# Joining the two output visits of a block on TensorE: chunked scan and gated MLP on one core

## The chip, the core and the metric

One core of a Trainium2 chip runs the whole program. The metric is device time in microseconds (us) for one execution; lower is better. Three runs of the kernel before took 336.29, 338.03 and 337.85 us, median 337.85.

## What is computed

A decayed linear-attention scan over 4 batches, 8 heads, 768 positions, head size 32 and state size 16 is followed by a gated MLP over the 3072 tokens (256 wide, 1536 hidden), all in float32. Cut to what matters:

```python
for c in range(nc):                      # chunks of 32 in the reference, pieces of 64 in the kernel
    cum = np.cumsum(la, axis=-1)
    L = np.exp(cum[:, :, :, None] - cum[:, :, None, :]) * causal
    M = np.einsum('bhin,bhjn->bhij', Cc, Bc) * L
    y_intra = np.einsum('bhij,bhjd->bhid', M, xc)
    y_inter = np.einsum('bhin,bhnd->bhid', Cc, state) * np.exp(cum)[:, :, :, None]
    y[:, :, sl] = y_intra + y_inter
    state = decay_full[:, :, None, None] * state + np.sum(Bx, axis=2)
...
g = x @ w_gate
return (g * sigmoid(g) * (x @ w_val)) @ w_out
```

## The kernel before, in words

The 768 positions are six blocks of 128 (numbered `k` from 0 in the code, so block two is `k == 1`), each of two pieces of 64. For a block, decays, B, C and x are loaded; VectorE scans the decays into `L` and `E`; TensorE computes state sums (`sums`) and scores (`scores`), in one visit for blocks two to five; VectorE multiplies scores by decays (`mix`) and carries the state on (`step`); then TensorE computes the block's outputs (`outputs`, which is `values`, decayed values from `L` and `x`, and then `carried`, the carried state against C). The result goes into four PSUM banks `y` and is copied out as the MLP's input, split into a high and a low part because the wide matmuls run in a reduced float32 form with two parts for each operand.

The outputs of a batch are 32 passes of values (64 rows by 32 columns of the array, 64 columns moved) and 16 passes of carried state (32 by 64, 64 moved); a float32 matmul is two passes, each with a weight load of its own. A block has four batches: 128 and 64 passes, 192 in all. Before, `outputs` runs twice for a block, for batches 0 and 1 and for batches 2 and 3, with a pause of 2.6 us of planner time between, in which TensorE takes other work.

That other work is the MLP: for a block 12 groups of gate and value matmuls (`gv`, 512 columns) and 12 of output matmuls (`po`). Block four's groups 4 to 11 are `halved` and blocks five and six together form a `PAIR`, both with fewer multiplications by means of mixed weights (`ws`, `wos`), which the kernel makes on the chip (`mix_weights`, `mix_out`), writes to DRAM (`keep`) and fetches again (`fetch_mixed`, `fetch_out`).

The order of the work on every engine comes out of a list scheduler, `Plan`, that runs on the host: each operation has a cost, a rank (about its due time, smaller goes first), what it needs and which buffers it takes. The order of each engine, and of the SP queue that issues the DMAs, is then fixed. The settings that the change touches stand near the end of the file: `LEAD[k]` is how far ahead of its MLP work a block's scan is ranked (`z` in the code), `LATER` how late the first nine weights are cast, `MAKE` and `MAKE_STEP` when the mixed gate weights are made, `OUT_MAKE` and `OUT_STEP` the same for the output weights, `AHEAD` how far ahead of use mixed weights are fetched, and `URGENT` the rank of the copies and sums between the halved block's terms. `IDLE` gives dummy passes (`idle`) that write a bank nobody reads: 22 of 128 columns at the very start, and a few of 512 columns in block one.

All engine calls are recorded at one line (L202, a helper), so rows are told apart by their tiles: `y<-L,xb` is `values`, `y<-bc,T` is `carried`, `st` and `S` are state sums and scores, `rest` is a dummy.

Of the kernel before, what the change touches and what calls it, by code (L numbers as in the profile page):

```python
# [17 lines left out]
BATCH, H, S, D, N = 4, 8, 768, 32, 16  # L18
DM, DFF = 256, 1536
P = 128  # L20
# [4 lines left out]
T = BATCH * P  # L25
# [18 lines left out]
class Plan:  # L44
# [26 lines left out]
    def add(self, engine, cost, run, rank, needs=(), takes=(), uses=(), gives=None, kind=None, lag=0.0, rows=1.0, slack=0.0):  # L71
        engines = [(engine, cost)] if cost is not None else engine
        self.ops.append(Op(engines, run, rank, needs, takes, uses, gives, kind, lag, rows, slack))
# [139 lines left out]
def scan_moe_kernel(ctx: ExitStack, tc, rows, decays, bc, xb, wgv, wo, cst, out):  # L213
# [763 lines left out]
    def gate_val(k, f, m):  # L977
        t = hid.setdefault((k, f), {})["gv"[m]] = ps_mm.tile([P, T], F32, tag="mm", name=f"gv{k}_{f}_{m}")
        if not k and f < WHOLE:
            w = part[f]["w"].bitcast(F32).rearrange("p (a b c) -> p a b c", b=2, c=P)  # L980
# [59 lines left out]
    def idle(n, i):  # L1040

        if not n and not i:
            rest[0] = ps_at.tile([P, T], F32, tag="at", name="rest")
        c = T if n else P
        wide = dn.rearrange("p g t -> p (g t)").bitcast(BF16)[:, :c] if n else one[:, :c]
        te.matmul(rest[0][:, :c], one[:, :P], wide, start=True, stop=True)

# [11 lines left out]
    def do(f, *a):  # L1059
        return lambda *e: f(*a, *e)  # L1060
# [6 lines left out]
    add = plan.add  # L1067
# [4 lines left out]
    def units(k, n):  # L1072
        return GV * n - (GV - GVH) * max(n - HALVED.get(k, NF), 0)

    for k in range(NB):
        begin[k] = t
        if k == PAIR:
            begin[k + 1], begin_sum[k], begin_sum[k + 1] = t, t + PAIR_LAG, t + NF * (GVP + PO)
            break
        t += (units(k, NF) if k else WHOLE * PACE0 + (NF - WHOLE) * GV) + ATT  # L1080
        for i in (() if not k else (0, 1) if k == 1 else (k,)):
# [3 lines left out]
    def due(k, f=0):  # L1085

        if k in HALVED:
            return begin[k] + units(k, f)
        return begin[k] + f * (GV if k else PACE0) - (0 if k else max(f - WHOLE, 0) * (PACE0 - GV))

# [6 lines left out]

    for n, ranks in enumerate(IDLE):
        for i, r in enumerate(ranks):
            need = [("idle", n, i - 1)] if i else [("idle", n - 1, len(IDLE[n - 1]) - 1)] if n else []  # L1100
            if n:
                need = need + [(("S", 0, BATCH - 1), ("vals", 0), ("y", 0))[n - 1]]
            takes = [] if i or n else [("at", "rest")]
            c = T if n else P
            add("PE", 0.2133 * c / T, do(idle, n, i), r, need, takes=takes, uses=["rest"], gives=("idle", n, i), kind="r")


    for i in range(NW):
# [8 lines left out]
        add("DVE", 0.6, do(w_round, i), r - 3.3 if i else -0.94, [("shift", i), ("rest", i), *([] if i else [("ce", 0)])], uses=[("raw", i)], gives=("round", i))  # L1117
        early = WHOLE <= i < NF
        if i < NF and not early:
            r = due(1, i) - LATER  # L1120
        later = [("M", 1, NP - 1)] if i < WHOLE else []
        add([("Act", 0.525), ("DVE", 0.34)], None, do(w_high, i), r - 2.7, [("round", i), *later], gives=("wh", i))
        whole_done = [("gv", 0, i, m) for m in range(2)] if i < WHOLE else []
        add("DVE", 0.6, do(w_low, i), r - 1.5, [("wh", i), *whole_done], uses=[("w", i)], gives=("wl", i))
# [9 lines left out]
    for k in range(NB):  # L1134
        r = due(k)
        SLACK = min(k / 2, 1.0)
        z = -5 if not k else r + LEAD[k]
        L, E, BC, XB, CZ, TT = ("L", k), ("E", k), ("bc", k), ("xb", k), ("Cz", k), ("T", k)
# [16 lines left out]
        if not k:  # L1155
# [3 lines left out]
            for b in range(BATCH + 1):  # L1159
                for i in range(2 if b < BATCH else 1):  # L1160
# [7 lines left out]
                    need = [t, ("decays", 0), "dj"] + ([("scan0", b - last_one)] if i else []) + ([("M", 0, NP - 2)] if b == BATCH else [])  # L1168
# [15 lines left out]
        y = [("y", k, i) for i in range(2 * K)]  # L1184
        for bs in [(b,) for b in range(BATCH)] if not k else [range(BATCH)]:
            b, more = bs[-1], bs[0]
            n = len(bs)
            stb = st[:1] if k in ST_ONE else st
            bank = "mm" if k in ST_MM else "at"
            if k in JOINED:  # L1190
# [3 lines left out]
                need = [*(("bt", k, i) for i in bs), ("Cz", k)]  # L1194
# [11 lines left out]
        for q in range(0 if k else 1, len(st)):  # L1206
            need = [*before, ("E", k), ("ap", k, q)] + ([] if k or q > 1 else [("ap", k, 0), ("round", 2)])
            add("DVE", 0.785, do(step, k, q), z + (8 if k else 25) + q, need, uses=[] + ([("T", k - 1)] if k and not q else []), gives=("step", k, q))
            before = [("step", k, q)]
        uses = [L, E, XB, BC, *y, TT]  # L1210
# [3 lines left out]
        for g in range(0 if k else 2):  # L1214
            need = [("M", 0, p) for p in (2 * g, 2 * g + 1)]
            add("PE", 0.45, do(values, 0, range(BATCH), (g,)), -1.4 + 0.1 * g, need, takes=[("mm", y[2 * q + g]) for q in range(K)], uses=[L, XB, *y], gives=("vals", g), kind="f")
        if k:
            need = [*(("M", k, p) for p in range(NP)), ("ce", k), *steps]
            add("PE", 1.52, do(outputs, k, (0, 1)), z + 11, need, takes=[("at", i) for i in y], uses=y, gives=("y", k, 0), kind="f", slack=min(k - 0.5, 2.5))
            add("~", 2.6, lambda: None, z, [("y", k, 0)], gives=("pause", k))  # L1220
            add("PE", 1.52, do(outputs, k, (2, 3)), z + 11, [("pause", k)], uses=[L, *uses], gives=("y", k), kind="f")
        for b in range(0 if k else BATCH):
            add("PE", 0.135, do(carried, 0, b), -1, [("vals", 0), ("vals", 1), ("ce", 0), *steps], uses=uses, gives=("y", 0) if b == BATCH - 1 else ("y", 0, b), kind="f")
        done = [("y", k)]
# [71 lines left out]
    for r in range(NF // 2):  # L1296
        at = OUT_MAKE + OUT_STEP * r
        i = NF + r
        u = [("sg", ("out", r, n)) for n in range(2)]
        add("DVE", 0.6, do(whole_again, r), at, [("wl", i), ("wh", i), ("round", NW - 1), MIXED_AFTER, *prior], takes=u, gives=("ws", i, -1))  # L1300
        uses = [key for _, key in u]
# [6 lines left out]
    for k in (*HALVED, PAIR):  # L1308
        for f in user(k):
            other = in_raw(f) if k == PAIR else f in LOOSE.get(k, ())  # L1310
            need = [("spared", f), *behind, *(["new_t1", "new_t2"] if other and k == PAIR else [("xtl", k, 1)] if other else [])]
# [9 lines left out]
    def stay_home(r, n):  # L1321
        home = HOMES[r][STAYS.index(n)]
        if home == "sg":
            return [("sg", ("stay", r, n))], []
        if home[0] == "wg":
            return [], [("term", home[1], i) for i in (1, 2, 4)]
        return [], [("spare", *home[:2])]
# [4 lines left out]
    for f in range(NF):  # L1332
        r = due(PAIR, f)
        c = 0.681
# [25 lines left out]
        for b in range(2):  # L1360
            home, need = stay_home(f // 2, f"{f % 2 + 1}{b + 1}")
# [3 lines left out]
    for r in range(R):  # L1365
        at = due(PAIR, 2 * r + 1) + SUM_LAG
        pr = [("pr", PAIR + b, 2 * r + o) for b in range(2) for o in range(2)]
        for n, (t, *_) in enumerate((("t1",), ("t3",), ("t2",), ("t4",))):
            home, need = stay_home(r, t) if t != "t3" else ([], [])
            add("DVE", 0.6, do(stay_sum, r, n), at + n * 0.1, [*(pr if not n else [("ksum", r, n - 1)]), *need], takes=home, gives=("ksum", r, n))  # L1370

    at = due(PAIR) + 60.0
# [6 lines left out]
    for j, (n, r) in enumerate(first):  # L1379
        x = TERMS[n][0]  # L1380
        need = [("ksum", r, {"11": 0, "t3": 1, "t1": 2, "22": 2}.get(x, 3)), *([("split", j - 1)] if j else [])]
        tag = "sg" if j % (HB + MORE) >= HB else None
        lh = ("lh", r, x)
        takes = [("sg", lh), ("sg", (lh, 2))] if tag else [("hh", lh)]
# [11 lines left out]
    for j, (n, r, h) in enumerate(steps):  # L1396
# [3 lines left out]
        need = [("lh", r, x), ("ll", r, x), *gate[n], *([prev] if prev else []), *([("osum", r)] if n not in (1, 2, 4) else [])]  # L1400
        takes = [("at", tile_of[b])] if n in (1, 5) and not r or b == "q" and r == R - 2 else []
        uses = [tile_of[b]]
# [10 lines left out]
    for n, k, m, c0, c1, need in (("x", PAIR, 0, 0, T, (2, end, None)), ("z", PAIR + 1, 0, 0, T, (3, end, None)), ("y0", PAIR, 1, 0, T // 2, (4, end, 0))):  # L1413
        c = 0.6 * (c1 - c0) / T
# [47 lines left out]
    for k in range(NB):  # L1462
# [3 lines left out]
        for f in range(NF):  # L1466
            r = due(k, f)
            need = [*xs, ("wh", f), ("wl", f)]
            c = 1.362
            if not k:  # L1470
                need = [("round", f), *(("xf", i) for i in range(2 * K)), ("idle", len(IDLE) - 1, len(IDLE[-1]) - 1)]
                c = 1.717
                if f >= WHOLE:
                    need = [("wh", f), ("wl", f), *(("xh", 0, g) for g in range(2)), *(("xl", 0, g) for g in range(2))]
                    c = 1.362
# [20 lines left out]
        for n, (m, t, fs) in enumerate(sums_of(k) if k < PAIR else []):  # L1496
            b = ("po", k, m, t)
            need = [x for f in fs for x in (("hl", k, f), *([("hl", k, f, 0)] if in_halves(k, f) else []), ("wh", NF + f // 2), ("wl", NF + f // 2))]
# [3 lines left out]
            c = (0.681 if t[1] - t[0] == T else 0.71) * len(fs) * (t[1] - t[0]) / T  # L1502
            add("PE", c, do(project, k, m, t, fs), r, need, takes=[] if fs[0] else [("mm" if k < PAIR else "at", b)], uses=[b, *(("h", k, f) for f in fs)], gives=prev, kind="r")
            if fs[-1] == NF - 1:
                o = ("ob", k, m, t)
                c = 0.6 * (t[1] - t[0]) / T
# [5 lines left out]

CST = W + 2 + 2 * D + 2 * P
NA = NB * K * BATCH * H // P
IDLE = [-9.0] * 22, [-1.45] * 4, [-1.35] * 2, [1000.0] * 3
LATER = 2.4
ST_ONE, ST_MM, JOINED = (), (1, 2, 3, 4), (1, 2, 3, 4)
LEAD = {1: -26.4, 2: -36, 3: -65.3, 4: -66.7, 5: -56.2}
PAIR_LAG, MIXED, RAW = 5.0, 4, 4
MIXED_AFTER = ("y", 1)  # L1520
HALVED = {3: 4}
HALF_AT = "z"
MAKE, MAKE_STEP = 116.9, 3.3
LOOSE = {3: (3, 5, 7)}
AHEAD, URGENT = 14.6, 60


def in_raw(f):
    return f >= MIXED and f % 2 == 0


OUT_MAKE, OUT_STEP = 198.7, 3.7
OUT_RAW = 1, 3, 5
BEHIND, AFTER = 0.9, 0
MORE = 3
# [18 lines left out]
def in_halves(k, f):  # L1554
    return f >= HALVED.get(k, NF)


WHOLE = 9
LATE = {2: NF + 2}
GATE, HASTE = dict(bc=0, aj=0, xb=0, an=1), 7  # L1560
# [53 lines left out]
```

## Time and profile before

| what | us |
|---|---|
| profiled execution, its own time | 335.66 |
| its span, first to last instruction | 333.9 |
| TensorE matmul busy | 328.6 |
| VectorE busy | 295.4 |
| ScalarE busy | 193.4 |
| three runs | 336.29, 337.85, 338.03 |

The profile is of one execution. Busy times of engines lie beside each other; TensorE's weight loads are counted apart and overlap its matmuls. A matmul's duration runs from its start to its modelled end, and many small ones are under way at once, so the distance between starts says more than a duration.

### The profile page before, as it was taken

How to read it: one execution, taken by the hardware profiler on the slowest of the kernel's cores; microseconds unless marked ns; L12 is line 12 of the kernel's file. 1: busy time of each engine (PE TensorE's matmuls, PEld its weight loads, DVE VectorE, ACT ScalarE, POOL GpSimd, SP SyncE). 2: the span in 40 equal slices, each digit the busy share in tenths (PEclk: the TensorE clock that was granted, in tenths of full speed). 3: DMA queues.
4: the chain of work that ended last, by engine and by line, in shares of the span. 5: the costliest groups of instructions: out<-in, count | busy, mean ns of one | idle time of the engine just before them, and what ended most of it. 6: DMA issues, size and time to landing. Idle time of an engine off the chain costs nothing.

```text
span 333.9 us, 7899 instructions
## 1 busy us (share of the span) xinstructions
PE 328.6 (98%) x3186; PEld 258.4 (77%) x3189; DVE 295.4 (88%) x576; ACT 193.4 (58%) x359; POOL 4.1 (1%) x11
## 2 busy tenths in 40 slices
PE   8999999999999999999999999999999999999996
PEld 7644548888888888878888889998888888888785
DVE  6999999987997999888999975998578999989994
ACT  3696898275554653454454445543565556554982
POOL 1300000000000000000000000000000000000000
PEclk9999999999999999999999999999999999999999
DMA  7789659992001598378977489443046511330011
GB/s 249 269 266 340 196 158 381 296 240 52 14 33 34 166 281 345 102 279 234 293 228 291 168 275 222 160 132 125 2 127 251 191 57 71 125 126 0 1 66 63
DMA packets 21261, 57.68 MB, mean 173 GB/s; under 512 B 2280, under 2 KB 3304, under 8 KB 21224
## 3 DMA queue, kind: packets, MB, share of 16 engines
q1 hardware_dynamic: 20808, 56.94, 52.6%
q8 instruction: 25, 0.41, 0.5%
q10 hardware_dynamic: 416, 0.23, 0.2%
q14 instruction: 12, 0.10, 0.1%
HBM read 41.23 MB, written 15.93 MB: 171 GB/s over the span
## 4 chain that ended last, share of the span: by engine, by line
PE 96%; DMA 1%; ACT 1%; issue 0%; DVE 0%; SPq 0%; DVEq 0%; ACTq 0%
PE gv L202 35%; PE po L202 20%; PE py L202 7%; PE y L202 5%; PE px L202 5%; PE oy L202 4%; PE hy L202 3%; PE pz L202 2%; PE pr L202 2%; PE ox L202 2%; PE S L202 2%; PE hz L202 2%; PE hx L202 2%; DMA bc<-in_bc 1%; PE st L202 1%; PE oz L202 1%
## 5 line engine op out<-in xcount | busy, mean ns | idle before, releaser
L202 ACT CAST hh<-sg 128x512 fp32r<-128x512 f32 (+1 forms) x54 | 29.3, 558 | 33.2 <-PE po L202 24.2
L202 DVE TENSOR_TENSOR hl<-sg,hh 128x512 fp32r<-128x512 f32 (+1 forms) x56 | 33.7, 616 | 7.8 <-ACT hh L202 7.3
L202 ACT ACTIVATE sg<-gv 128x512 f32<-128x512 f32 x40 | 23.7, 593 | 24.6 <-PE gv L202 21.3
L202 DVE TENSOR_TENSOR sg<-gv,sg 128x512 f32<-128x512 f32 x40 | 27.5, 687 | 3.2 <-PE gv L202 3.2
L202 DVE TENSOR_TENSOR_SCAN L<-L,dj 128x520 f32<-128x520 f32 x20 | 24.2, 1232 | 0.0
L202 DVE TENSOR_TENSOR ws<-ws 128x128 f32<-128x128 f32 (+1 forms) x60 | 20.2, 369 | 0.1
L202 DVE TENSOR_TENSOR L<-S,L 128x512 f32<-128x512 f32 x24 | 15.8, 689 | 1.1 <-PE S L202 1.1
L202 ACT ACTIVATE sg<-px 128x512 f32<-128x512 f32 x12 | 7.2, 599 | 15.7 <-PE px L202 15.7
L202 PE MATMUL py<-xht,ws 128*128 128x512 f32 x48 | 15.3, 400 | 0.0
L202 DVE TENSOR_TENSOR hlt<-stt,hht 128x512 fp32r<-128x512 f32 x18 | 11.7, 690 | 0.9 <-ACT hht L202 0.7
L202 PEld LDWEIGHTS y<-L,xb 64*32 64x32 f32 x768 | 8.7, 105 | 4.6 <-issue 3.4
L202 ACT ACTIVATE sg<-pz 128x512 f32<-128x512 f32 x12 | 7.2, 599 | 7.2 <-PE pz L202 7.2
L202 ACT ACTIVATE Cz<-bc,cs 128x512 f32<-128x512 f32 x12 | 8.0, 717 | 5.2 <-DMA bc<-in_bc 5.2
L202 ACT CAST ws<-ws 128x512 fp32r<-128x512 f32 x11 | 6.9, 623 | 7.1 <-DVE ws L202 7.0
L202 PE MATMUL y<-L,xb 64*32 64x64 f32 x768 | 10.8, 224 | 0.1
L202 PEld LDWEIGHTS py<-xht,ws 128*128 128x128 f32 x48 | 8.6, 188 | 2.7 <-DVE pz L202 1.2
L202 DVE TENSOR_TENSOR ps<-py,ps 128x512 f32<-128x512 f32 x12 | 8.3, 690 | 2.6 <-PE py L202 2.6
L202 ACT CAST hht<-stt 128x512 fp32r<-128x512 f32 x17 | 9.8, 621 | 0.7 <-DVE stt L202 0.6
L202 PE MATMUL py<-xlt,ws 128*128 128x512 f32 x24 | 9.3, 389 | 0.0
L202 DVE TENSOR_TENSOR pz<-py,ps 128x512 f32<-128x512 f32 x12 | 8.3, 696 | 0.6 <-PE py L202 0.3
L202 ACT COPY py<-px 128x512 f32<-128x512 f32 x12 | 6.9, 574 | 1.3
L202 PE MATMUL y<-bc,T 32*64 32x64 f32 x352 | 7.6, 223 | 0.0
(788 smaller groups left out, 978.8 us busy)
## 6 DMA issues: line engine op xcount, KB each, us to landing
ws<-keep SPq DMA_DIRECT2D x20, 512.0 KB, 4.2
keep<-ws SPq DMA_DIRECT2D x12, 512.0 KB, 6.3
L<-clipped SPq DMA_DIRECT2D x10, 520.0 KB, 9.5
xb<-in_xb SPq DMA_DIRECT2D x6, 768.0 KB, 7.7
bc<-in_bc SPq DMA_DIRECT2D x6, 512.0 KB, 9.7
ws<-uncut SPq DMA_DIRECT2D x12, 256.0 KB, 3.9
wos_k<-keep SPq DMA_DIRECT2D x6, 512.0 KB, 4.3
out<-ob SPq DMA_DIRECT2D x8, 256.0 KB, 2.9
```

The source lines that it names most:

```text
L202: ins = getattr(self.engine, name)(*a, **k)
```

## The change

Blocks two, four, five and six (`MERGED = 1, 3, 4, 5`) compute their outputs of all four batches in one planned operation of 192 passes: 128 of values, then 64 of carried state. Block three keeps two visits with the pause. The dummies at the start are 17 of 164 columns. Eight settings have new values.

```diff
-        c = T if n else P
+        c = T if n else WARM[1]
...
-            add("PE", 1.52, do(outputs, k, (0, 1)), z + 11, need, takes=[("at", i) for i in y], uses=y, gives=("y", k, 0), kind="f", slack=min(k - 0.5, 2.5))
-            add("~", 2.6, lambda: None, z, [("y", k, 0)], gives=("pause", k))
-            add("PE", 1.52, do(outputs, k, (2, 3)), z + 11, [("pause", k)], uses=[L, *uses], gives=("y", k), kind="f")
+            takes = [("at", i) for i in y]
+            if k in MERGED:
+                add("PE", 2.64, do(outputs, k, range(BATCH)), z + 11, need, takes=takes, uses=[L, *uses], gives=("y", k), kind="f", slack=min(k - 0.5, 2.5))
+            else:
+                add("PE", 1.52, do(outputs, k, (0, 1)), z + 11, need, takes=takes, uses=y, gives=("y", k, 0), kind="f", slack=min(k - 0.5, 2.5))
+                add("~", 2.6, lambda: None, z, [("y", k, 0)], gives=("pause", k))
+                add("PE", 1.52, do(outputs, k, (2, 3)), z + 11, [("pause", k)], uses=[L, *uses], gives=("y", k), kind="f")
...
-IDLE = [-9.0] * 22, [-1.45] * 4, [-1.35] * 2, [1000.0] * 3
-LATER = 2.4
+WARM = 17, 164
+IDLE = [-9.0] * WARM[0], [-1.45] * 4, [-1.35] * 2, [1000.0] * 3
+LATER = 3.7
-LEAD = {1: -26.4, 2: -36, 3: -65.3, 4: -66.7, 5: -56.2}
+LEAD = {1: -26.4, 2: -36.0, 3: -72.0, 4: -78.0, 5: -56.2}
-MAKE, MAKE_STEP = 116.9, 3.3
+MAKE, MAKE_STEP = 114.2, 3.3
-AHEAD, URGENT = 14.6, 60
+AHEAD, URGENT = 12.5, 50.5
-OUT_MAKE, OUT_STEP = 198.7, 3.7
+OUT_MAKE, OUT_STEP = 208.5, 5.4
+MERGED = 1, 3, 4, 5
```

## Rows read from the trace of the kernel before

**Rows 1.** The page, parts 1 and 2: busy times, and granted clock in 40 slices.

```profile
PE 328.6 (98%) x3186; PEld 258.4 (77%) x3189; DVE 295.4 (88%) x576; ACT 193.4 (58%) x359; POOL 4.1 (1%) x11
...
PEclk9999999999999999999999999999999999999999
```

**Rows 2.** The page, part 4: chain that ended last, shares by engine.

```profile
PE 96%; DMA 1%; ACT 1%; issue 0%; DVE 0%; SPq 0%; DVEq 0%; ACTq 0%
```

**Rows 3.** The chain in order of time: start us, us, what.

```profile
55.97 36.95 PE gv L202 x162
...
144.01 1.41 PE y L202 x85
145.42 4.31 PE gv L202 x18
149.73 1.41 PE y L202 x85
```

**Rows 4.** TensorE's timeline about block three's second half visit: start us, us, what.

```profile
109.24 0.39 PE L202 MATMUL po<-hh,wo4l 128*128 128x512 f32 x1
109.56 0.86 PE L202 MATMUL y<-L,xb 64*32 64x64 f32 x64
110.34 0.69 PE L202 MATMUL y<-bc,T 32*64 32x64 f32 x32
110.97 0.50 PE L202 MATMUL po<-hh,wo4h 128*128 128x512 f32 x1
111.31 0.39 PE L202 MATMUL po<-hl,wo4h 128*128 128x512 f32 x1
```

**Rows 5.** The tile y: its two kinds of matmul, min/median/max ns.

```profile
L202 PE MATMUL y<-L,xb x768: 212/216/240, 11.4 to 238.1; 64*32 64x64 f32 x192
...
L202 PE MATMUL y<-bc,T x352: 217/217/265, 13.8 to 238.7; 32*64 32x64 f32 x176
```

**Rows 6.** TensorE's timeline, block three's scores and the pass behind.

```profile
95.00 1.21 PE L202 MATMUL S<-Cz,bc 32*64 32x128 f32 x64
96.13 0.50 PE L202 MATMUL po<-hh,wo0h 128*128 128x512 f32 x1
```

**Rows 7.** TensorE's timeline, first half visits of blocks two and five.

```profile
48.63 0.99 PE L202 MATMUL y<-L,xb 64*32 64x64 f32 x64
...
188.81 0.95 PE L202 MATMUL y<-L,xb 64*32 64x64 f32 x64
```

**Rows 8.** TensorE's timeline at the start.

```profile
0.82 2.50 PE L202 MATMUL rest<-const-bfloat16-1.0 128*128 128x128 bf16 x22 [0.82 <-PEq L1603]
3.51 4.20 PE L202 MATMUL a<-rows 128*128 128x260 f32 x16 [0.19 <-DVE rows L202]
```

**Rows 9.** Waits of the SP queue: who waited for whom, us, times, longest.

```profile
SPq L202 <- PE y L202: 8.0, 3, 4.8
```

**Rows 10.** The page, part 6: DMA issues, KB each, median us to landing.

```profile
ws<-keep SPq DMA_DIRECT2D x20, 512.0 KB, 4.2
...
L<-clipped SPq DMA_DIRECT2D x10, 520.0 KB, 9.5
...
out<-ob SPq DMA_DIRECT2D x8, 256.0 KB, 2.9
```

**Rows 11.** Busy time by stretch: us, PE, PEld, DVE, ACT, POOL, PEclk, DMA share, GB/s.

```profile
180.00:190.00 10.00, 10.00 (x152) 8.03 (x143) 10.00 (x29) 4.02 (x9) 0.00 (x0) 1.00 0.34 126
...
200.00:210.00 10.00, 10.00 (x76) 9.51 (x75) 5.96 (x10) 4.58 (x9) 0.00 (x0) 1.00 1.05 242
```

**Rows 12.** VectorE's timeline, first scan and last product of block five.

```profile
165.52 1.24 DVE L202 TENSOR_TENSOR_SCAN L<-L,dj 128x520 f32<-128x520 f32 x1
...
185.38 0.70 DVE L202 TENSOR_TENSOR L<-S,L 128x512 f32<-128x512 f32 x1
```

**Rows 13.** The page, part 3: TensorE's instruction queue, packets, MB, share of 16 engines.

```profile
q8 instruction: 25, 0.41, 0.5%
```

**Rows 14.** Busy time by stretch, in block one (columns as in rows 11).

```profile
8.00:12.00 4.00, 3.77 (x182) 2.76 (x183) 4.00 (x8) 1.74 (x5) 2.87 (x5) 1.00 0.48 155
```

More of the change, by code (lines that the diff above doesn't have):

```diff
@@ L1103, in scan_moe_kernel @@
             takes = [] if i or n else [("at", "rest")]
-            c = T if n else P
+            c = T if n else WARM[1]
             add("PE", 0.2133 * c / T, do(idle, n, i), r, need, takes=takes, uses=["rest"], gives=("idle", n, i), kind="r")
```

## The prediction

> **What bounds the kernel now.** I read the page from the top down to single passes. Part 1 comes first: TensorE is busy for 328.6 of 333.9 us, and the granted clock stands at its upper level in every slice [rows 1]. The chain that ended last says the same: 96% of it is TensorE, next to no wait [rows 2]. So a change pays if it takes time out of the sequence of passes itself, and it costs if it makes that sequence wait. In order of time the chain shows wide work without a seam, 162 passes in 36.95 us (0.228 us each), cut by the outputs of a block: 1.41 us, 4.31 us of wide work, 1.41 us again [rows 3]. These pairs are what the change joins.
>
> The timeline of one such half visit shows what it costs [rows 4]. The last wide pass ahead of the visit is followed after 0.32 us, 0.09 more than the usual 0.228, and the first one behind it after 0.34 us, 0.11 more. Inside are 64 passes of decayed values and 32 of the carried state. One pass lasts 0.216 or 0.217 us [rows 5], far longer than the distance between starts, so starts have to be counted: the 64 begin between 109.56 and 109.56+0.86-0.216 = 110.20, 0.64 us or 10.0 ns each; the 32 begin between 110.34 and 110.34+0.69-0.217 = 110.81, 0.47 us or 14.7 ns each. Between the kinds nothing starts for 0.14 us, and none for 0.16 us before the wide work resumes. That is 0.64+0.14+0.47+0.16 = 1.41 us.
>
> **The change, part by part.**
>
> *One visit for two, blocks two, four, five and six.* No pass goes away: 192 stay 192. What goes is one run-in and run-out and two changeovers. A merged visit takes 128 x 10.0 ns + 0.14 + 64 x 14.7 ns + 0.16 = 1.28+0.14+0.94+0.16 = 2.52 us, where two halves take 2.82: 0.30 us less inside. At the outside one 0.09 and one 0.11 go: 0.20 us. Together 0.50 us a block, 2.0 us for four. All of it is on the path, since no engine but TensorE is on it. Bounds: the passes of the second half need not keep 10.0 and 14.7 ns in so long a row, and the nearest row of a longer one is the joined visit of state sums and scores, whose 64 score passes, of twice the columns, take 96.13-95.00 = 1.13 us, 17.7 ns each [rows 6]. With all 96 added passes at that pace (1.70 us where 0.64+0.47 = 1.11 was counted) the gain of a block becomes a loss of 0.09 us, 0.4 us in all. Upwards, the added 64 values could be a fifth faster, 0.13 us a block: 2.5 us. I take 2.0, as every undisturbed half visit of the trace has the same 1.41 us.
>
> Two of the visits start before their inputs are all there: 0.99 and 0.95 us for the 64 where 0.86 is usual [rows 7], 0.22 us together. The merged visit needs the same inputs at its start, so these stay: 0. The half visits were apart by a forced pause; the products behind them (four banks copied and split) waited for the second half, so they come earlier now, never later.
>
> *The dummies.* 22 passes of 128 columns (2816) become 17 of 164 (2788); at 2.50 us for the 22, one per cent less, and they end near 3.3 us, while the next TensorE work starts at 3.51 [rows 8] released by VectorE's clipping of the rows. Nothing: that wait covers it. Without the cover it would be the 0.02 us that one per cent makes, so no clock effect is seen in it. Ten TensorE instructions fewer (a weight load and a matmul for each of five) stand ahead of everything.
>
> *The settings.* Block four's whole preparation moves 6.7 us up in the ranks, block five's 11.3: for each, on SP two decay loads, the decay row load and the loads of B, C, x; on VectorE five scans, five weighings, four products, eight state steps; the joined TensorE visit of 1.9 us; six ScalarE operations; then the outputs. SP issues these ahead of weight transfers that it used to send first. What sets their earliest moment is the single buffer of decays: SP waits for TensorE's outputs to release it [rows 9], the load takes 9.5 us [rows 10], then come the scans. Merging and the earlier rank release it some 11 us sooner after block four (6.7 of rank and the 4.31 of wide work), and block six can follow. On TensorE order alone changes, at no cost. VectorE is the cover to watch: it is busy 10.00 of 10 us at 180 to 190, but 5.96 at 200 to 210 [rows 11]. Block five's work there, first scan at 165.52 and last product at 185.38 [rows 12], moves to about 154 to 174; the mixing of the output weights, ranked 9.8 us later and spread over steps of 5.4 instead of 3.7, makes the room. I cost this at 0; without the room three gate products of 0.70 us late would be 2.1 us.
>
> The mixed weights are fetched 2.1 us later, 12.5 us ahead of use, and land in 4.2 [rows 10]: 8.3 us left, 0; without that, 0.5 to 4 us once. Making them 2.7 us earlier and casting nine weights 1.3 us earlier moves work off no bound: the 162 passes that use the nine run without a gap [rows 3]. The seeds and forks of the halved block still rank 50.5 us before they are due, ahead of all else: 0; if one slipped behind a 0.70 us operation in each of four rounds, 2.8 us.
>
> **Sum.** The profiled execution took 335.66 us (span 333.9, 1.76 around it): less 2.0 is 333.7. That execution lies below the three runs (336.29, 337.85, 338.03), the median 2.19 above it. The middle of the four times is 337.07; less 2.0 it is 335.1, and the median less 2.0 is 335.85. I forecast 335.4 us, which puts no change at 337.4; the rivals' times go from there.
>
> **The rivals.**
>
> *A: the code does not come fast enough (slower).* TensorE's instructions arrive by a queue of their own: 25 packets, 0.41 MB, 0.5% of 16 engines' span, so 1.07 us a packet [rows 13]. 6375 recorded weight loads and matmuls over 25 packets are 255 for each. A visit of 192 passes is 384 instructions: it contains one border of packets always and, where it stands unluckily (half of all places), two, 256 instructions or 1.3 to 1.9 us apart. Present visits of 192 and 256 instructions can hardly hold two, so no row shows such a case. If a packet is asked for only at the border before, and needs 1.07 us, it is hidden; if it needs what the quickest store of 256 KB takes to land, 2.9 us [rows 10], each unlucky visit waits 1.2 us on average (2.9 less 1.7). The point from which it decides is 1.7+0.5 = 2.2 us for a packet. All four unlucky: 4.8 us against 2.0, 2.8 slower than now, 340.2; two of four: 337.8, no difference. For it: visits of blocks four and five move by 60 and 100 instructions, places that no row gives. Against it: half of the places are safe, and a packet's own 1.07 us is less than the shortest distance of 1.3.
>
> [...]
>
> *B: order (about even).* VectorE, full from 160 to 190, delivers gate products or split halves late once block five's work moves into that stretch, and TensorE waits. For it: its share there. Against: it is free for 4 us of the ten behind 200, and only deferrable weight work needs to give way. 2.1 us of waits takes the gain: 337.5; with the halved block's 2.8 as well, 340.3.
>
> *C: only the outer edges go.* The added passes run slower than the first ones by what the changeovers give: 4 x 0.20 = 0.8 us, 336.6. Nothing excludes it, and the lower bound above is near.
>
> That the granted clock falls in a 2.5 us stretch of small passes has no chance of its own: in block one 182 passes, most of them small, fill four microseconds at a granted clock of 1.00 [rows 14].
>
> **How the numbers follow.** Forecast 0.54; A 0.16, of which 0.07 slower and 0.09 no difference; B 0.16, of which 0.05 slower, 0.09 no difference and 0.02 faster all the same; C 0.14, no difference. A measurement of this kernel can tell about 0.5% from no change, 1.7 us. Faster 0.54+0.02 = 0.56, no difference 0.09+0.09+0.14 = 0.32, slower 0.12. The range goes from the profiled time with the upper bound, 335.66-2.5 = 333.2, to B's 337.5 and A's 337.8 with half a microsecond for the spread of the runs, 338.3; the slower cases, 0.12, stay outside. Faster alone would be 333.2 to 336.1.
>
> **What would show it.** Right: four output visits of some 2.5 us in the chain, the 128 values starting over 1.28 us and the 64 carried over 0.94, one 0.32 and one 0.34 at the edges, block three as before, TensorE's busy time down by 2 us. Wrong: a hole inside a visit that neither VectorE nor ScalarE releases (A); gaps in the wide work between 150 and 240 us released by VectorE (B); 2.6 us and more for the visit without a hole (C); dummies that end after 3.51 us or a slice of the clock under 9.

## The result: slower by 0.8%, and the profile after

The changed kernel takes 339.67 us (median of 11 runs, 337.71 to 341.26), the kernel before 337.04 on the same chip (11 runs, 335.82 to 338.03): ratio 1.0079, with a 95% interval of 1.0060 to 1.0097. The forecast was 335.4 with a range of 333.2 to 338.3, so it failed in sign. The profiled execution took 340.25 us, its span 338.5, 4.6 us more than that of before.

First the page, parts 1 and 2, of the kernel after. It answers to [rows 1].

```profile
PE 328.6 (97%) x3181; PEld 259.3 (77%) x3184; DVE 296.4 (88%) x576; ACT 192.1 (57%) x359; POOL 4.1 (1%) x11
...
PEclk9999997999999999999999999999999999999999
```

TensorE is busy for exactly as long as before while the span grew by 4.6 us: time went into holes, stretches in which TensorE starts nothing. In one slice, the seventh (51 to 59 us), the granted clock is no longer at its upper level (7 in the row, 9 in all others). Then the chain in order of time (start us, us, what), which answers to [rows 3]:

```profile
149.11 2.51 PE y L202 x155
151.62 2.05 PE gv L202 x8
...
189.31 2.51 PE y L202 x155
...
193.78 12.70 DMA bc<-in_bc
206.50 1.34 ACT Cz L202 x2
```

The merged visits of blocks four and five (and six, at 232.19) last 2.51 us each, as forecast (2.52). But behind block four's visit eight wide passes are done at 153.67 and the next piece of the chain starts at 154.11, and at 193.78 the chain leaves TensorE: block six's load of B and C took 12.70 us, `Cz` on ScalarE came late, and a copy queued behind it held up `hy`. TensorE's timeline shows the places (start us, us, instruction, count, what the idle time before ended with); its first two rows answer to [rows 8], the third stands in block one's outputs:

```profile
0.82 2.48 PE L202 MATMUL rest<-const-bfloat16-1.0 128*128 128x164 bf16 x17 [0.82 <-PEq L1609]
3.48 4.23 PE L202 MATMUL a<-rows 128*128 128x260 f32 x16 [0.17 <-DVE rows L202]
...
13.13 0.33 PE L202 MATMUL y<-L,xb 64*32 64x64 f32 x10 [0.57 <-issue]
...
49.53 1.81 PE L202 MATMUL y<-L,xb 64*32 64x64 f32 x128
51.28 1.16 PE L202 MATMUL y<-bc,T 32*64 32x64 f32 x64
52.37 0.73 PE L202 MATMUL gv<-xh,wg9h 128*128 128x512 f32 x2
55.74 1.22 PE L202 MATMUL gv<-xh,wg9l 128*128 128x512 f32 x2 [2.64 <-DVE wg11w L202]
56.76 0.63 PE L202 MATMUL gv<-hhx,wg9h 128*128 128x512 f32 x1
57.18 0.63 PE L202 MATMUL gv<-hlx,wg9h 128*128 128x512 f32 x1
...
59.21 0.40 PE L202 MATMUL gv<-hhx,wg9h 128*128 128x512 f32 x1
59.45 0.40 PE L202 MATMUL gv<-hlx,wg9h 128*128 128x512 f32 x1
...
149.04 1.49 PE L202 MATMUL y<-L,xb 64*32 64x64 f32 x128
150.46 1.16 PE L202 MATMUL y<-bc,T 32*64 32x64 f32 x64
151.55 0.73 PE L202 MATMUL gv<-xh,wg4h 128*128 128x512 f32 x2
...
153.04 0.62 PE L202 MATMUL gv<-xh,wg4h 128*128 128x512 f32 x2
154.11 0.63 PE L202 MATMUL gv<-xh,wg4l 128*128 128x512 f32 x2 [0.44 <-issue]
```

Inside block four's visit all is as the forecast had it: values from 149.04, carried from 150.46, wide work from 151.55, 2.51 us in all. Behind block two's visit two wide passes start, the next one only at 55.74; from the start of the second (52.70) that is 3.04 us instead of 0.23. From there wide passes start 0.42 us apart (56.76, 57.18), until at 59.21 and 59.45 the distance is 0.24 again. Eight passes take 59.21-55.74 = 3.47 us where 8 x 0.228 = 1.82 is usual. The windows view has the cause of that (us, PE, PEld, DVE, ACT, POOL with counts, granted clock, DMA share, GB/s; as [rows 11]):

```profile
52.70:55.74 3.04, 0.40 (x3) 0.00 (x1) 3.04 (x7) 2.69 (x7) 0.00 (x0) 0.99 1.06 356
55.66:59.07 3.41, 3.33 (x8) 2.69 (x9) 0.69 (x3) 1.17 (x3) 0.00 (x0) 0.50 0.90 334
59.10:62.50 3.40, 3.40 (x16) 2.77 (x16) 2.56 (x5) 2.65 (x6) 0.00 (x0) 1.00 1.01 391
...
0.00:55.70 55.70, 50.19 (x723) 27.90 (x726) 50.78 (x102) 40.94 (x77) 4.14 (x11) 1.00 0.76 251
0.00:154.08 154.08, 148.12 (x1741) 107.93 (x1745) 136.65 (x278) 93.96 (x176) 4.14 (x11) 0.99 0.62 198
```

Behind this hole, with no pass started for 3 us, the granted clock is 0.50 for 3.4 us where it is 1.00 in the stretch behind (59.10 to 62.50): a second price of the hole, 3.47-1.82 = 1.6 us. Of the 11 runs 7 have a mean granted clock of 0.995 or less (median 339.91 us) and 4 one of 1.000 (median 338.88), so most runs seem to pay it. The last two rows count what TensorE had started when the holes ended, 723+726 = 1449 and 1741+1745 = 3486 instructions; the experiments come back to these numbers.

The waits (engine, tile, for whom: us, times, longest) name several causes:

```profile
PE gv L202 <- DVE wg11w L202: 2.6, 1, 2.6
...
PE hy L202 <- ACT hy L202: 0.6, 1, 0.6
...
PE gv L202 <- issue: 0.4, 1, 0.4
```

The first, by far the largest, is put down to VectorE, the last to nothing ("issue": the profile shows no wait). The balance of the spans, from starts in the two traces: merging -2.0; the first wide pass behind block one at 16.04 instead of 15.13, +0.9 (this start lies between 15.0 and 16.1 in the runs below; 0.5 of the 0.9 is the hole at 13.13, which is 0.25 us long in the trace of before and 0.77 here, the rest a later `Cz`); block two's visit, whose inputs came late, +0.2; the hole behind it +2.8 and the lower clock +1.6; the hole behind block four's +0.6; the late `hy` +0.6. That is +4.7, against 338.5-333.9 = 4.6.

So two questions: what makes the holes (VectorE, as the wait says, or the arrival of code, rival A), and what else the settings cost.

### The profile page after: what moved, and what is told of

It is laid out like the page before. It is cut to its first block, busy times and chain, and to the rows that moved or that the text cites. A ratio compares the mean times of both kernels' runs of the same rounds, so it can differ in the third digit from the quotient of the medians.

```text
span 338.5 us, 7894 instructions
## 1 busy us (share of the span) xinstructions
PE 328.6 (97%) x3181; PEld 259.3 (77%) x3184; DVE 296.4 (88%) x576; ACT 192.1 (57%) x359; POOL 4.1 (1%) x11
## 4 chain that ended last, share of the span: by engine, by line
PE 78%; DMA 4%; ACT 1%; DVE 0%; issue 0%; DVEq 0%
PE gv L202 23%; PE po L202 18%; PE py L202 7%; PE px L202 5%; DMA bc<-in_bc 4%; PE oy L202 4%; PE y L202 3%; PE hy L202 3%; PE pz L202 2%; PE pr L202 2%; PE ox L202 2%; PE hx L202 1%; PE hz L202 1%; PE S L202 1%; PE oz L202 1%; PE or L202 1%
## 5 line engine op out<-in xcount | busy, mean ns | idle before, releaser
L202 PE MATMUL y<-L,xb 64*32 64x64 f32 x768 | 9.9, 225 | 0.7 <-issue 0.6
L202 PE MATMUL S<-Cz,bc 32*64 32x128 f32 x384 | 7.2, 278 | 0.7 <-ACT Cz L202 0.7
L202 ACT COPY ps<-pr 128x512 f32<-128x512 f32 x12 | 7.1, 588 | 1.0
```

What stands on the lines that cost most here:

```text
L202: ins = getattr(self.engine, name)(*a, **k)
```

## The experiments

Each run stands beside runs of the kernel before on the same chip. Each edit is shown against the changed kernel or the kernel before, as named.

**1. all_split**: the changed kernel, no visit merged.

```diff
-MERGED = 1, 3, 4, 5
+MERGED = ()
```

> Changed kernel with its dummies and settings, but every block's outputs in two visits. Code theory (instructions come in packets of 256, and a visit of 384 reaches the end of the second packet before the third is there): no hole behind the outputs of blocks two and four, so 2 to 4 us less than the changed kernel, but not better than the kernel before: +0.5 to +1.5 us on it, from the slower start (0.9 us) and the wait for the copy of the halved block (0.8 us). Order theory (the settings make VectorE deliver late): the hole of 2.8 us at the low part of weight 9 stays, and the time stays 2 to 3 us over the kernel before, plus the 2 us that merging gave.

Measured: 338.94 us, ratio 1.0085 (1.0056 to 1.0114). The holes at 1449 and 3486 instructions and the half clock are gone, as the code theory said; its time (0.5 to 1.5 us over the kernel before) was missed, for the time is hardly better than with merging (four runs). The settings and dummies, costed at nothing, cost 338.94-336.33 = 2.6 us. This does not add up with the balance above, where the visits and their holes make 3.0 us and all else 1.7: the waits of `gv` for `sg` and of `hy` for `hz` below stand in this kernel's profile and not in that of the changed kernel. The three largest of the waits of TensorE on other engines in this run that the kernel before does not have (another 0.2 us is of `hx` for ScalarE):

```profile
PE y L202 <- DVE L L202: 0.7, 1, 0.7
PE gv L202 <- ACT sg L202: 0.7, 1, 0.7
...
PE hy L202 <- DVE hz L202: 0.3, 1, 0.3
```

**2. merge_alone**: the kernel before with the four visits merged (the planner's code for it is that of the change), dummies and settings untouched.

```diff
+MERGED = 1, 3, 4, 5
```

> Kernel before with the merged visits of blocks two, four, five and six as the only edit; 22 dummies of 128 and the old settings. The next border of packets falls 5 instructions ahead of the end of block two's visit, 7 behind that of block four, 37 and 40 behind those of blocks five and six. Code theory: a hole of 2.5 to 4 us at the end of block two's visit, one of 0.6 to 3 us behind block four's, none behind five and six, so the kernel is slower than before by 1 to 4 us. Order theory: without the new settings there is no hole and the kernel is 2.0 us faster than before.

Measured: 340.54 us, ratio 1.0125 (1.0060 to 1.0190), four runs: merging alone makes the kernel slower, about as much as the whole change does (the two intervals overlap). TensorE's timeline about block two's visit:

```profile
49.97 1.15 PE L202 MATMUL y<-bc,T 32*64 32x64 f32 x61
54.16 0.27 PE L202 MATMUL y<-bc,T 32*64 32x64 f32 x2 [3.04 <-issue]
```

Its windows view, counting from the span's start to the end of each hole:

```profile
0.00:54.10 54.10, 49.38 (x723) 27.68 (x726) 50.13 (x101) 40.03 (x74) 4.24 (x11) 1.00 0.77 258
0.00:152.27 152.27, 146.91 (x1741) 107.32 (x1745) 136.54 (x279) 95.10 (x175) 4.24 (x11) 0.99 0.63 199
```

The hole (3.2 us) is now inside the visit, between two passes of the carried state that wait for no other engine, and no engine releases it. It stands at 723+726 instructions, to the instruction where it stood in the changed kernel, and a second (0.8 us) at 1741+1745. VectorE's `wg11w` in the wait above was only what happened to end last. The distance of the two places, 3486-1449 = 2037, is 8 x 256 less 11, and 11 is the number of TensorE's semaphore instructions between them, which this view does not count. Packets of TensorE's own queue hold 16 KB, 255 recorded instructions on average [rows 13]; the distance says 256. Below, a border is a place in TensorE's stream of instructions where one packet ends and the next begins.

**3 and 4. dummies11, dummies28**: the changed kernel with 11 dummies of 253 columns or 28 of 100, which moves the same borders six passes later or eleven earlier in the work.

```diff
-WARM = 17, 164
+WARM = 11, 253      # dummies28: 28, 100
```

> Changed kernel with 11 dummies of 253 columns for 17 of 164: the same columns, the same order behind them, 12 instructions fewer ahead of everything. Code theory: every border comes 12 instructions (6 wide passes, 1.4 us) later in the work: the hole behind block two's visit stands 6 passes further on and is some 1.4 us shorter, the 0.6 us behind block four's is gone, and 1.5 to 3.5 us are won on the changed kernel. Order theory: the same hole at the same pass, no change of time.

> Changed kernel with 28 dummies of 100 columns: 22 instructions more ahead of everything. Code theory: the hole of block two moves into its visit, among the last 9 of the carried-state passes, which wait for no other engine there, and grows by some 1 us to 3 to 4.5; block four's hole stands 4 instructions behind its visit and is 1 to 3 us. Order theory: the hole stays at the low part of weight 9 with the length it had.

Measured: 337.40 us, ratio 1.0032 (1.0009 to 1.0056), for 11 dummies; 346.26 for 28, a single run, of which only the trace is used here. The order of all other work is the same in the three kernels on every engine, and in both the hole goes with the count, not with the work. With 11, TensorE's timeline behind block two's visit:

```profile
53.50 0.61 PE L202 MATMUL gv<-xh,wg9h 128*128 128x512 f32 x2
55.47 0.50 PE L202 MATMUL gv<-xh,wg9l 128*128 128x512 f32 x1 [1.36 <-issue]
```

and the count at the end of that hole, in the windows view:

```profile
0.00:55.40 55.40, 51.68 (x723) 28.50 (x726) 50.66 (x102) 41.31 (x79) 4.19 (x11) 1.00 0.77 252
```

Six wide passes more are done before the hole, which shrinks from 2.8 to 1.5 us, by the 6 x 0.228 = 1.4 us that they take; block four's is gone; the clock does not fall. But block five's visit, whose border now stands 27 instructions ahead of it, has a hole of 1.3 us. With 28, TensorE's timeline about the visits of blocks two and four:

```profile
52.46 1.04 PE L202 MATMUL y<-bc,T 32*64 32x64 f32 x55
56.59 0.37 PE L202 MATMUL y<-bc,T 32*64 32x64 f32 x2 [3.10 <-issue]
...
153.13 1.15 PE L202 MATMUL y<-bc,T 32*64 32x64 f32 x61
156.76 0.27 PE L202 MATMUL y<-bc,T 32*64 32x64 f32 x2 [2.49 <-issue]
```

and the counts at the ends of the holes, in the windows view:

```profile
0.00:56.50 56.50, 49.09 (x723) 27.61 (x726) 50.42 (x101) 39.84 (x73) 4.16 (x11) 0.99 0.75 245
0.00:156.70 156.70, 146.78 (x1741) 107.38 (x1745) 134.85 (x273) 92.96 (x171) 4.16 (x11) 0.98 0.62 195
```

The same two counts, now inside both visits, 3.3 and 2.7 us, with the granted clock at 0.50 behind each (for 6.8 and 3.4 us), and a third hole of 2.1 us in block one. That settles the instruction's place in the stream as the cause, against VectorE.

**5 and 6. old_56_d22, old_56_d18**: the kernel before with only blocks five and six merged, whose borders lie well; with its own dummies, or with 18 of 156 columns.

```diff
+MERGED = 4, 5
-IDLE = [-9.0] * 22, ...      # old_56_d18 alone
+WARM = 18, 156               # old_56_d18 alone
```

> Kernel before with the merged visits of blocks five and six alone; old settings, 22 dummies of 128. By the count of recorded instructions a border of packets falls 165 and 162 instructions into these visits, the next one 37 and 34 behind their ends (some 18 wide passes, 4 us). Code theory: no hole, each visit 2.5 us, so 1.0 us faster than the kernel before (0.3%), +-0.5. Rival (any visit of 192 passes brings a hole of its own): 1 to 4 us slower.

> The same with 18 dummies of 156 columns, borders at 173 and 170 and the next ones 45 and 42 behind the visits. Code theory: also 1.0 us faster than before, no difference to 22 dummies beyond 0.4 us in block one. Rival: as above.

Measured: 336.03 us against 336.59, ratio 0.9974 (0.9954 to 0.9995), with 22 dummies: 0.6 us faster by the medians and 0.9 by the ratio, where two blocks at 0.50 should give 1.0; the interval reaches from 0.2 to 1.5. No hole at a border behind either visit. This is the only version whose interval lies below the kernel before. With 18 dummies 336.92, ratio 0.9993 (0.9968 to 1.0019): no holes there either, yet the gain doesn't show; block one has a hole of 0.46 us at a border that the profile of the other lacks, the rest lies within the intervals.

**7 and 8. split_later, split_lead**: all_split with one setting back at its old value: `LATER` (in the code a larger value ranks the casts of the first nine weights earlier), or the lead of blocks four and five.

```diff
-LATER = 3.7                                  # split_later alone
+LATER = 2.4
-LEAD = {..., 3: -72.0, 4: -78.0, 5: -56.2}   # split_lead alone
+LEAD = {..., 3: -65.3, 4: -66.7, 5: -56.2}
```

> All visits split, new settings, but the nine weights cast at the old rank (2.4 for 3.7). If the earlier casts are what makes block two's last score product late, the hole of 0.9 us inside its first visit falls to some 0.1 and the time to 0.8 us under that of the all-split kernel; if not, no change.

> All visits split, new settings, but blocks four and five led by the old 65.3 and 66.7. If moving their preparation is what costs, the hole of 0.9 us at 180 us and those of 0.4 and 0.5 at 220 to 225 go, 1 to 2 us less than the all-split kernel; if they come from the changed weight steps (made earlier, output weights later, fetched and copied later), no change.

Measured: split_later 339.02, ratio 1.0061 (1.0037 to 1.0084), no better than all_split within the intervals: TensorE's wait for `L` in block two falls from 0.7 to 0.3 us, and one of 0.5 for the cast of `wg2w` comes in its place. split_lead 337.74, ratio 1.0030 (1.0008 to 1.0052), 1.2 us less than all_split by the medians and 1.8 by the ratios. Of TensorE's waits the three that all_split has behind 180 us are gone, and one of `gv` for VectorE (at 160 us) has come:

```profile
PE gv L202 <- DVE sg L202: 0.6, 1, 0.6
```

**9 and 10. dummies_only, other_settings**: the kernel before with 17 dummies of 164 and nothing else; or with all new settings but the lead and the dummies. No visit is merged.

```diff
+WARM = 17, 164                                # dummies_only
...
+LATER = 3.7                                   # other_settings, from here on
+MAKE, MAKE_STEP = 114.2, 3.3
+AHEAD, URGENT = 12.5, 50.5
+OUT_MAKE, OUT_STEP = 208.5, 5.4
```

> The kernel before with 17 dummy passes of 164 columns in place of its own, all visits in two halves, all other settings as before. Theory (the settings' 2.6 us lie in the order, not in the dummies): the same as before within 0.5 us, ratio 0.9985 to 1.0015. Rival (moving the borders by five passes puts them where a split visit crosses them badly): some 1 us slower, ratio 1.003, with a hole at an instruction index 256 j - 66 that the kernel before does not have.

> The kernel before with the changed kernel's settings of the order except the lead of the visits (that one and the dummies as before), all visits in two halves. Theory (the lead costs most of the settings' 2.6 us, the rest of the settings the remaining 1 us): 0.5 to 1.2 us slower than before, ratio 1.0015 to 1.0035. Rival (the remainder is the dummies'): the same as before within 0.4 us. A second rival (the rest of the settings costs as much as the lead): 2 us slower or more, ratio 1.006.

Measured: dummies_only 337.62 us against 336.62, ratio 1.0033 (1.0009 to 1.0057): the theory of this run fell, its rival holds. The dummies alone cost about 1.1 us. Block one crosses a border inside its outputs (instruction 441) and starts there lie 0.76 us apart, 0.27 in the profile of before; over all profiles it is 0.5 to 0.8 with 17 dummies and 0 to 0.5 with 22. The remaining 0.6 us stays unexplained. The profile's largest wait, 0.7 us in block two for VectorE's `L`, does not explain it, since profiles of kernels with 22 dummies have it too (0.3 in old_56_d22, 0.7 in other_settings). other_settings 337.61, ratio 1.0016 (0.9997 to 1.0034): 1.0 us by the medians and 0.5 by the ratio, within the expected band, though the interval still touches none.

**11. old_456**: the kernel before with blocks four, five and six merged, block four's visit placed to lie well to the borders.

```diff
+MERGED = 3, 4, 5
+... slack=0.3 if k == 3 else min(k - 0.5, 2.5)
```

> The kernel before with the visits of blocks four, five and six merged, block four's placed so that the packet border inside it stands 159 instructions behind its beginning (165 and 168 for five and six), the dummies and settings of before left as they were. Theory (the hole comes only where the next border stands less than some 30 instructions behind the visit's end, and merging itself is worth 0.5 us a block): no hole of over 0.4 us at or behind the three visits, each of about 2.5 us, and 1.5 us faster than before, give or take 0.5, ratio about 0.9955. Rival (any merged visit risks a hole wherever it stands, or the gain is taken back by a late sum): a hole again behind block four's visit, or no gain: ratio 0.999 to 1.005.

Measured: 336.89 us against 336.62, ratio 1.0007 (0.9990 to 1.0024). The first half of the expectation held: TensorE's timeline shows no hole behind block four's visit (nor behind five's and six's).

```profile
142.51 1.49 PE L202 MATMUL y<-L,xb 64*32 64x64 f32 x128
...
145.02 0.73 PE L202 MATMUL gv<-xh,wg3h 128*128 128x512 f32 x2
...
148.32 0.61 PE L202 MATMUL gv<-xh,wg4l 128*128 128x512 f32 x2
```

The second half, 1.5 us gained, did not. The waits say where it went; the kernel before has neither of these two:

```profile
PE hz L202 <- DVE L L202: 0.7, 1, 0.7
...
PE hy L202 <- DVE hz L202: 0.3, 1, 0.3
```

TensorE waits for VectorE's products and seeds at 215 and 220 us (1.26 us by the starts). The three kernels with the old settings and block four merged (merge_alone, old_456, old_456_d32) all have the wait of `hz`, and old_56_d22, with block four split, has not; that the changed order behind block four makes it is the likely reason.

**12. old_456_d32**: old_456 with 32 dummies of 88 columns, as many columns as 22 of 128; the order of all other work is the same on every engine, and only twenty TensorE instructions more stand ahead of it.

```diff
-WARM = 22, 128
+WARM = 32, 88
```

> The kernel old_456 with 32 dummy passes of 88 columns in place of 22 of 128: the same 2816 columns, the same operations in the same order on every engine, only twenty TensorE instructions more ahead of all the rest. They move the packet border inside the merged visits of blocks four, five and six from 159, 165 and 168 to 139, 145 and 148 instructions behind the visit's beginning, and the next border from 31, 37 and 40 instructions behind the visit's end to 11, 17 and 20. Theory (the hole comes of the borders' places alone): a hole of 0.4 to 1.6 us behind each of the three visits, at the instruction where the next packet begins, which old_456 does not have, and perhaps one of up to 2 us in block one at about 17 us, where a border comes to stand 9 instructions behind its outputs: 1.5 to 6 us slower than old_456, ratio to the kernel before 1.005 to 1.018. Rival (the holes come of the order of the work or of its inputs): no such holes, the same time as old_456 within 0.7 us, ratio 0.999 to 1.003.

Measured: 338.56 us, ratio 1.0057 (1.0031 to 1.0082), 1.7 us slower than old_456. In TensorE's timeline, where old_456 has none, holes stand in block one and behind block four's visit:

```profile
15.52 0.67 PE L202 MATMUL gv<-xf,wg0w 128*128 128x512 f32 x1
18.03 1.55 PE L202 MATMUL gv<-xf,wg0w 128*128 128x512 f32 x3 [1.84 <-issue]
...
146.81 0.40 PE L202 MATMUL gv<-xl,wg3h 128*128 128x512 f32 x1
147.79 0.50 PE L202 MATMUL gv<-xl,wg3h 128*128 128x512 f32 x1 [0.58 <-issue]
```

and the windows view counts, up to the end of the second hole:

```profile
0.00:147.75 147.75, 144.14 (x1744) 104.39 (x1744) 134.48 (x274) 91.81 (x171) 4.16 (x11) 1.00 0.66 202
```

2.1 us at 15.5 and 0.75 us at 1744+1744 = 3488 instructions. The order is identical, so place alone makes these holes, and the rival (order or inputs) falls. But the expectation of one behind each of three visits failed: block five's shows some 0.2 us and block six's none, with borders at nearly the same place in the visit (145 and 148 against 139). The bound is not sharp: in the table below the packet begins 0.8 to 4.7 us behind the crossing.

**What the holes have in common.** Counting recorded TensorE instructions in the traces gives the moment at which the previous border was crossed, and the records of the instruction queue the moment at which the packet's transfer began (the border's place is known to about three instructions; with TensorE's semaphore instructions counted in, 21 of them ahead of 1449 and 32 ahead of 3486, all borders lie 256 apart):

| kernel, block | previous border crossed, us | packet begins | TensorE goes on | hole, us |
|---|---|---|---|---|
| before, one | 8.83 | 9.65 | 12.22 | 0.25 |
| changed, one | 9.24 | 10.47 | 13.13 | 0.77 |
| changed, two | 50.48 | 53.44 | 55.74 | 2.8 |
| changed, four | 149.75 | 151.65 | 154.11 | 0.6 |
| merge_alone, two | 49.13 | 51.67 | 54.15 | 3.2 |
| merge_alone, four | 148.87 | 149.84 | 152.32 | 0.8 |
| dummies11, two | 50.17 | 53.13 | 55.47 | 1.5 |
| dummies11, five | 182.43 | 185.14 | 188.00 | 1.3 |
| dummies28, two | 51.56 | 54.10 | 56.59 | 3.3 |
| dummies28, four | 152.29 | 154.46 | 156.76 | 2.7 |
| dummies28, one | 12.64 | 17.37 | 19.57 | 2.1 |
| old_456_d32, one | 12.21 | 15.76 | 18.03 | 2.1 |
| old_456_d32, four | 143.93 | 145.51 | 147.79 | 0.75 |

From the packet's beginning to the restart it is 2.2 to 2.9 us in all thirteen. At none of the other borders in the fourteen traces does the first instruction behind it start sooner than 2.1 us after its packet began. The packet itself begins 0.8 to 4.7 us behind the crossing. Together 3.4 to 6.9 us pass at these holes from one border to the first instruction behind the next, and in that time TensorE starts the 256 instructions between the two and no other. Wide passes take 0.11 us an instruction (0.228/2), so 256 last 29 us (from 262.70 to 292.07 between two borders in the trace of before); a merged visit takes 2.51 us for 384. At the holes a visit and the wide passes beside it run through the 256 in less than those 3.4 to 6.9 us. The split visits of before have no such hole, with wide work between the halves: the 256 instructions up to 1449 take 6.1 us there, those up to 3486 5.9.

## Why the prediction failed, point by point

**The merged visit: right.** 2.52 us forecast, 2.51 measured in three blocks, with the values' starts over 1.27 us, the carried ones over 0.94, and 0.32 and 0.34 at the edges of blocks four and five; none of the bounds of [rows 6] was needed, and rival C (only the outer edges go) did not occur. That the 0.50 us a block reach the whole time is shown only once (old_56_d22, 0.6 to 0.9 us for two blocks); old_56_d18 and old_456 show no gain.

**Rival A: named, but mis-sized, and this is the first step that failed.** The prediction let it decide "at 2.2 us for a packet", priced a packet at 1.07 or at most 2.9 us counted from the border, and let only a visit with two borders inside suffer. The sum of the forecast has it at nothing; in the changed kernel holes and lower clock cost 2.8+1.6+0.6 = 5.0 us behind the merged visits. The 2.2 to 2.9 us of the table are near that upper figure, but they count from the packet's beginning, which lies another 0.8 to 4.7 us behind the border. With 3.4 us and more in all, a visit with its next border 5 (block two) or 17 instructions (block four) behind its end is hit as well: neither hole of the changed kernel stands inside a visit. "Half of the places are safe" was too kind; in these runs borders some 157 to 217 instructions into the visit were free of holes, those at 111 to 139 were not, those at 144 to 150 went both ways, and the one at 229 (dummies11, block five, with another border 27 ahead of the visit) had a hole. The row that decides stood in the trace of before: in block one TensorE starts nothing from 11.94 to 12.22, at a border whose packet began at 9.65, so 2.57 us and not 1.07 pass from a packet's beginning to its first instruction, above the 2.2 from which rival A decides. TensorE's timeline of before on both sides of it:

```profile
11.46 0.70 PE L202 MATMUL y<-L,xb 64*32 64x64 f32 x47
...
12.22 0.34 PE L202 MATMUL y<-L,xb 64*32 64x64 f32 x15
```

And the price left out what follows a hole of 3 us: 3.4 us at a granted clock of 0.50. [rows 14] had been read as excluding a fall of the clock. That was right for the dense passes here: in the changed kernel the granted clock is 1.00 in block two's visit (49.80 to 52.30) and falls only at the end of the stop, at 55.66.

How many packets TensorE holds at once no view shows. What the traces show is that the packet for the instruction counted 1449 begins, in the changed kernel, at 53.44, 2.96 us after the border 256 instructions ahead has been passed (50.48), and that in all thirteen rows of the table a packet begins behind that crossing. With holes of up to 3.3 us the fetch was not hidden there. The prediction held the packet's own 1.07 us against rival A, which was the wrong row.

**The settings at nothing: the second failed step.** all_split shows 2.6 us for all of them and the dummies. The parts, each in a run of its own: lead 1.2 to 1.8, dummies 1.1, the rest 0.5 to 1.0 (the intervals of the ratios are 0.6 to 1.0 us to either side, and the three parts need not add up). Rival B had this mechanism, VectorE's and ScalarE's work late behind 180 us, at 2.1 us; but it got 0.16, and stood for itself where it came together with A. The argument for the lead, that block five's work "moves to about 154 to 174", did not come true in the profile after, VectorE's timeline:

```profile
166.78 1.23 DVE L202 TENSOR_TENSOR_SCAN L<-L,dj 128x520 f32<-128x520 f32 x1
...
185.43 0.69 DVE L202 TENSOR_TENSOR L<-S,L 128x512 f32<-128x512 f32 x1
```

First scan 166.78 and last product 185.43, against 165.52 and 185.38 before [rows 12], while TensorE's work there stood some 5 us later. The step that failed is that decays would be released "some 11 us sooner": SP issues block five's decay load right behind block four's outputs, at 151.41 before, 152.28 after, 152.83 in all_split and 152.77 in split_lead, whatever the rank. And where only the lead differs, the earlier rank is the later one: the last product stands at 192.95 in all_split and at 187.40 in split_lead. Which work it pushed in front of the block was not traced.

**The dummies at nothing.** Their end (3.30 us, next work at 3.48) is as forecast. What they changed is not their time but their count: with ten instructions fewer block one waits at its border 0.5 us longer in the profiles compared, about half of the 1.1 us; the other half is open. The prediction noted the ten instructions and drew nothing from them.

## What to carry to other kernels

In these runs time saved by packing small matmuls densely counted only where their code arrived in time: merge_alone, with holes of 3.2 and 0.8 us, has a ratio of 1.0125 to the kernel before, old_56_d22, with none behind its merged visits, 0.9974. So find the borders of packets in the trace (here 256 instructions apart; holes that no engine releases, at the same count in several kernels), and keep enough work between two of them (at the holes here 3.4 to 6.9 us passed from a border to the first instruction behind the next). A wait that the profile puts down to an engine is worth a check by a run in which that engine has nothing to do with it. A planner's settings that look free in every row can still cost as much as the change gains, so run the old settings with the new part before tuning them anew.

## What the runs showed of the hardware beyond what was expected

- At the holes, a border crossed in dense small passes was followed by the start of the next packet 0.8 to 4.7 us later, and by the first instruction out of it after 2.2 to 2.9 more. In wide work the packet mostly begins before the border is crossed (0.7 to 1.9 us before it at the last three borders of the kernels before and after); block one's wide passes are an exception, where it begins 17 us behind the third border (19.38 and 36.79 in the trace of before) and still comes in time. Why a packet comes late was not settled, but the traces point at other DMA traffic. At the border in block six's outputs it begins 0.7 to 0.8 us behind the crossing in the six traces in which the DMA engines are nearly idle there (share 0.03 or 0.04 in the two us about it), and 1.6 to 2.1 us in the eight in which they are busy (0.83 to 0.95). No run changed the traffic alone.
- Behind the holes of 2.7 to 3.3 us, in which TensorE stood still, the granted clock was 0.50 for 3.4 us, once for 6.8 (dummies28, behind block two); behind the shorter ones, up to 2.1 us, it stayed at 1.00.
- Ten or twenty instructions at the very start moved the time of the whole kernel by 1.1 us (dummies_only) and 1.7 us (old_456_d32), with all other work in the same order on every engine.
